# Rebuilding the last stage of a backward kernel: where dh1 is summed, when dQ and dVK are reloaded, who computes the LayerNorm backward, and when the dmod part runs

## The chip, the cores and the metric

The kernel runs on one core of one Trainium2 chip. The metric is the time of one execution on the device, in microseconds (us). A time is the median of a number of executions, which is given with it ("median of 3 runs"). The engines are PE (matmul), DVE (vector), ACT (scalar), POOL (GpSimd) and SP (which here only issues transfers). In this program PE writes its sums to tiles in PSUM; the other tiles on the chip lie in SBUF. A profile is one execution seen by the hardware profiler; its span is up to 12 us away from the median of the timed runs, so times are compared between timed runs, and stages between profiles. The kernel before took 3349.34 us (median of 3 runs, 3345.37 to 3352.89) before the change was tried.

## The reference

The program computes a transformer block with adaptive LayerNorm (attention with 32 heads of width 16, then an MLP with squared ReLU) on 2048 tokens of width 512, and then all its gradients. Cut to what the change touches:

```python
mod = (_silu(c) @ w_mod).reshape(c.shape[0], 6, 1, -1)       # sa, ca, ga, sb, cb, gb
h = _layernorm(x, axis=-1) * (1 + ca) + sa
x = x + ga * _A_ref(h, A_wqkv, A_wo)                          # attention: qkv = h @ wqkv, ...
h = _layernorm(x, axis=-1) * (1 + cb) + sb
x = x + gb * _B_ref(h, B_w1, B_b1, B_w2, B_b2)
...
_out, _vjp = jax.vjp(_f, A_x, A_wqkv, A_wo, B_w1, B_b1, B_w2, B_b2, c, w_mod)
```

The last stage of the backward pass has dQ, dK and dV of all heads and must still make five things: dh1 = dQKV · wqkvᵀ (2048 x 512), the LayerNorm backward of dh1 (which gives dx, an output, and two row sums for the gradients of sa and ca), dWqkv = h1ᵀ · dQKV, dW_mod (an outer product, 512 x 3072) and dc (which needs w_mod transposed).

## The kernel before

The attention backward walks over 8 head groups of 4 heads. It leaves dQ of a head group as a tile of 128 x 2048 (channels on the partitions, padded) in DRAM, and dV and dK together as another. The stage after that loop, which I call the tail, read them back one head group at a time:

```python
stgJ = ph.enter_context(tc.tile_pool(name="phJs", bufs=1))
...
for hg in range(HG):                                # 8 head groups
    xs = []
    for t3 in range(2):                             # dQ, dVK
        xt = stgJ.tile([P, n], BF, name=f"xst{t3}", tag=f"xst{t3}")
        SP.dma_start(out=xt[:], in_=srcs[t3][hg])
        xs.append(xt)
    for qt in range(TT):                            # 16 token tiles
        pt = pst.tile([P, 2, P], BF, name="ptq", tag="ptq")
        for t3 in range(2):
            PE.transpose(pt[:, t3, :], xs[t3][:, qt * P:(qt + 1) * P], identb[:])
        for t3 in range(3):                         # token-major dQ, dK, dV
            ...                                     # ACT copies dQ, DVE copies dK and dV
        pd = psd.tile([P, D], F32, name="pdh1", tag="pdh1")
        for t3 in range(2):
            PE.matmul(pd[:], xs[t3][:, qt * P:(qt + 1) * P], wT_pad[:, t3 * 8 + hg, :],
                      start=(t3 == 0), stop=(t3 == 1))
        if hg == 0:
            ACT.activation(dh1acc[:, qt, :], pd[:], AF.Identity)
        else:
            DVE.tensor_tensor(dh1acc[:, qt, :], dh1acc[:, qt, :], pd[:], ALU.add)
for t in range(TT):                                 # LayerNorm backward, all of it on DVE
    ...
    DVE.tensor_tensor_reduce(out=dxn1[:], in0=dh1acc[:, t, :], in1=ca1_bc, ...)
    DVE.tensor_tensor_reduce(out=prod1[:], in0=dxn1[:], in1=xn1[:], ...)
    PE.matmul(prow_sa[0:1, :], ones_bf[:, 0:1], dxn1[:], start=(t == 0), stop=(t == TT - 1))
    PE.matmul(prow_ca[0:1, :], ones_bf[:, 0:1], prod1[:], start=(t == 0), stop=(t == TT - 1))
    ...                                             # six more DVE operations, store of dx
...
SP.dma_start(out=h1J[:], in_=h1_st[:])              # then dWqkv: 192 matmuls
...                                                 # then the dmod part:
SP.dma_start(out=out_9.rearrange("(ic p) j -> p ic j", p=P), in_=dwmod_sb[:])   # 3 MB
for jc in range(24):
    SP.dma_start(out=wmodT[:, jc, :], in_=w_mod[:, jc * P:(jc + 1) * P], transpose=True)
```

Of the kernel before, what the change touches and what calls it, by code (L numbers as in the profile page):

```python
# [15 lines left out]
ALU = mybir.AluOpType  # L16
# [6 lines left out]
DC = 4  # L23
# [11 lines left out]
def kernel(  # L35
# [653 lines left out]

    with ExitStack() as ph:  # L690
        strm = ph.enter_context(tc.tile_pool(name="phIs", bufs=2))
        ework = ph.enter_context(tc.tile_pool(name="phIe", bufs=4))
        tpool = ph.enter_context(tc.tile_pool(name="phIt", bufs=2))
        stg = ph.enter_context(tc.tile_pool(name="phIg", bufs=2))
# [66 lines left out]
        def v_quad(u):  # L761
            hg, kc, qc, qi = units[u]
            qt = qc * 4 + qi
            E_u, dS_u = bst.pop(u)
            acc = cur["vk"]
            for hq in range(4):
                PE.matmul(acc[32 * hq:32 * hq + DH, :], dOs_tok[:, qt, (hg * 4 + hq) * DH:(hg * 4 + hq + 1) * DH], E_u[:, hq, :],  # L767
                          start=False, stop=(qt == TT - 1), tile_position=(0, 32 * hq), skip_group_check=True)
            if qt == TT - 1:
                ACT.activation(hst[hg]["vk"][:, kc * 512:(kc + 1) * 512], acc[:], AF.Identity)  # L770
                if kc == QC - 1:
                    SP.dma_start(out=dVKtP[hg], in_=hst[hg]["vk"][:])

        def dq_quad(b, kt):
# [9 lines left out]
            if kt == 3:  # L784
# [13 lines left out]
                if kc == QC - 1 and qc == QC - 1:  # L798
                    SP.dma_start(out=dQtP[hg], in_=st["dq"][:])
# [4 lines left out]
        with tc.manual_schedule(engines={PE.engine, ACT.engine, DVE.engine}):  # L804
            for j in range(2 * NU + 10):
                u, pair, sub = j // 2, j % 2, j % 8
                if j < 2 * NU:
                    if pair == 0 and units[u][1:] == (0, 2, 0) and units[u][0] + 1 < HG:
                        load_head(units[u][0] + 1)
                    for hi in range(2):  # L810
# [14 lines left out]
    with ExitStack() as phq:  # L825
        bigJ = phq.enter_context(tc.tile_pool(name="phJbig", bufs=1))
        dqkv_tok = bigJ.tile([P, TT, 3 * D], BF, name="dqkv_tok")
        ph = ExitStack().__enter__()
        bigJ2 = ph.enter_context(tc.tile_pool(name="phJbig2", bufs=1))
        stgJ = ph.enter_context(tc.tile_pool(name="phJs", bufs=1))  # L830
        wk = ph.enter_context(tc.tile_pool(name="phJw", bufs=2))
        dh1acc = bigJ2.tile([P, TT, D], F32, name="dh1acc")
        x0_tok = bigJ2.tile([P, TT, D], BF, name="x0_tokJ")
        SP.dma_start(out=x0_tok[:], in_=x_dram)
        dx1_tok = bigJ2.tile([P, TT, D], BF, name="dx1_tokJ")
        SP.dma_start(out=dx1_tok[:], in_=dx1_st[:])
        with ExitStack() as ph2:
            pst = ph2.enter_context(tc.tile_pool(name="psJt", bufs=2, space=bass.MemoryType.PSUM))
            psd = ph2.enter_context(tc.tile_pool(name="psJd", bufs=2, space=bass.MemoryType.PSUM))
            srcs = (dQtP, dVKtP)  # L840
            for hg in range(HG):
                xs = []
                for t3 in range(2):
                    xt = stgJ.tile([P, n], BF, name=f"xst{t3}", tag=f"xst{t3}")
                    SP.dma_start(out=xt[:], in_=srcs[t3][hg])
                    xs.append(xt)
                for qt in range(TT):
                    pt = pst.tile([P, 2, P], BF, name="ptq", tag="ptq")
                    for t3 in range(2):
                        PE.transpose(pt[:, t3, :], xs[t3][:, qt * P:(qt + 1) * P], identb[:])  # L850
                    for t3 in range(3):
                        dst = dqkv_tok[:, qt, t3 * D + hg * 64:t3 * D + (hg + 1) * 64].rearrange("q (h d) -> q h d", h=4)
                        srcv = pt[:, 0 if t3 == 0 else 1, :].rearrange("q (h c) -> q h c", h=4)
                        srcv = srcv[:, :, DH:2 * DH] if t3 == 1 else srcv[:, :, 0:DH]
                        if t3 == 0:
                            ACT.activation(dst, srcv, AF.Identity)
                        else:
                            DVE.tensor_copy(dst, srcv)
                    pd = psd.tile([P, D], F32, name="pdh1", tag="pdh1")
                    for t3 in range(2):  # L860
                        PE.matmul(pd[:], xs[t3][:, qt * P:(qt + 1) * P], wT_pad[:, t3 * 8 + hg, :],
                                  start=(t3 == 0), stop=(t3 == 1))
                    if hg == 0:
                        ACT.activation(dh1acc[:, qt, :], pd[:], AF.Identity)
                    else:
                        DVE.tensor_tensor(dh1acc[:, qt, :], dh1acc[:, qt, :], pd[:], ALU.add)
        with tc.tile_pool(name="psJr", bufs=1, space=bass.MemoryType.PSUM) as psr:
            prow_sa = psr.tile([P, D], F32, name="prow_sa")
            prow_ca = psr.tile([P, D], F32, name="prow_ca")
            for t in range(TT):  # L870
                xn1 = wk.tile([P, D], BF, name="xn1b", tag="xn1b")
                DVE.tensor_scalar(xn1[:], x0_tok[:, t, :], mean1[:, t:t + 1], rstd1[:, t:t + 1], ALU.subtract, ALU.mult)
                dxn1 = wk.tile([P, D], BF, name="dxn1", tag="dxn1")
                s1 = wk.tile([P, 1], F32, name="s1a", tag="s1a")
                DVE.tensor_tensor_reduce(out=dxn1[:], in0=dh1acc[:, t, :], in1=ca1_bc, scale=1.0, scalar=0.0,
                                         op0=ALU.mult, op1=ALU.add, accum_out=s1[:])
                prod1 = wk.tile([P, D], BF, name="prod1", tag="prod1")
                s2 = wk.tile([P, 1], F32, name="s2a", tag="s2a")
                DVE.tensor_tensor_reduce(out=prod1[:], in0=dxn1[:], in1=xn1[:], scale=1.0, scalar=0.0,
                                         op0=ALU.mult, op1=ALU.add, accum_out=s2[:])  # L880
                PE.matmul(prow_sa[0:1, :], ones_bf[:, 0:1], dxn1[:], start=(t == 0), stop=(t == TT - 1))
                PE.matmul(prow_ca[0:1, :], ones_bf[:, 0:1], prod1[:], start=(t == 0), stop=(t == TT - 1))
                c1 = wk.tile([P, 1], F32, name="c1a", tag="c1a")
                DVE.tensor_scalar(c1[:], s1[:], 1.0 / D, None, ALU.mult)
                c2 = wk.tile([P, 1], F32, name="c2a", tag="c2a")
                DVE.tensor_scalar(c2[:], s2[:], 1.0 / D, None, ALU.mult)
                tq = wk.tile([P, D], BF, name="tqa", tag="tqa")
                DVE.tensor_scalar(tq[:], xn1[:], c2[:, 0:1], None, ALU.mult)
                uq = wk.tile([P, D], BF, name="uqa", tag="uqa")
                DVE.tensor_tensor(uq[:], dxn1[:], tq[:], ALU.subtract)  # L890
                vq = wk.tile([P, D], BF, name="vqa", tag="vqa")
                DVE.tensor_scalar(vq[:], uq[:], c1[:, 0:1], rstd1[:, t:t + 1], ALU.subtract, ALU.mult)
                dx0t = wk.tile([P, D], BF, name="dx0t", tag="dx0t")
                DVE.tensor_tensor(dx0t[:], dx1_tok[:, t, :], vq[:], ALU.add)
                SP.dma_start(out=out1_v[:, t, :], in_=dx0t[:])
            rowt2 = wk.tile([1, 2, D], F32, name="rowt_saca", bufs=1)
            DVE.tensor_copy(rowt2[:, 0, :], prow_sa[0:1, :])
            DVE.tensor_copy(rowt2[:, 1, :], prow_ca[0:1, :])
            SP.dma_start(out=rows_st[0:2, :].unsqueeze(0), in_=rowt2[0:1, :, :])
        ph.__exit__(None, None, None)  # L900
        bigJ3 = phq.enter_context(tc.tile_pool(name="phJbig3", bufs=1))
        wk = phq.enter_context(tc.tile_pool(name="phJw2", bufs=2))
        h1J = bigJ3.tile([P, TT, D], BF, name="h1J")
        SP.dma_start(out=h1J[:], in_=h1_st[:])
        with tc.tile_pool(name="psJw", bufs=1, space=bass.MemoryType.PSUM) as psw:
            for t3 in range(3):
                accs = [psw.tile([P, D], F32, name=f"awq_{ic}", tag=f"awq_{ic}") for ic in range(DC)]
                for t in range(TT):
                    for ic in range(DC):
                        PE.matmul(accs[ic][:], h1J[:, t, ic * P:(ic + 1) * P], dqkv_tok[:, t, t3 * D:(t3 + 1) * D],  # L910
                                  start=(t == 0), stop=(t == TT - 1))
                for ic in range(DC):
                    wblk = wk.tile([P, D], BF, name="wqblk", tag="wqblk")
                    ACT.activation(wblk[:], accs[ic][:], AF.Identity)
# [114 lines left out]
```

## Time and profile before

| stage, kernel before | us | length | what holds it |
|---|---|---|---|
| attention backward loop, end | 3047.4 | | last dQ sum on POOL |
| wait for the first reload | 3047 to 3062 | 14.5 | the last dQ goes out and comes back |
| transposes and dh1, 128 steps | 3062 to 3197 | 135 | see below |
| LayerNorm backward | 3197 to 3244 | 47 | DVE |
| wait for h1 | 3244 to 3254 | 10 | DMA |
| dWqkv | 3254 to 3300 | 46 | PE |
| dmod part | 3300 to 3345 | 45 | transfers, DVE, PE in turn |

The tail is 298 us. The page's first part (busy time and share of the span of each engine) doesn't show it, since the tail is 9% of the span:

```profile
PE 2615.0 (78%) x17549; PEld 775.1 (23%) x17549; DVE 2004.4 (60%) x2889; ACT 2151.9 (64%) x3457; POOL 442.9 (13%) x458
```

So the tail has to be read by stretches. Each row of the next view is one stretch of time: its length, then the busy time of each engine (and the count of its instructions), the granted PE clock (1.00 is full speed), the share of the DMA engines and the rate. It is the view by windows of the kernel before.

```profile
core 0: us, PE busy (x) PEld busy (x) DVE busy (x) ACT busy (x) POOL busy (x), PEclk, DMA share, GB/s
3062.00:3197.00 135.00, 101.16 (x512) 46.10 (x510) 94.44 (x367) 35.56 (x144) 0.00 (x0) 0.87 0.16 55
3197.00:3244.00 47.00, 18.10 (x32) 2.52 (x32) 47.00 (x177) 0.00 (x0) 0.00 (x0) 0.54 0.12 39
3244.00:3254.00 10.00, 0.30 (x1) 0.14 (x2) 8.30 (x7) 0.00 (x0) 0.00 (x0) 0.50 0.63 236
3254.00:3300.00 46.00, 43.90 (x192) 19.15 (x190) 0.00 (x0) 5.48 (x11) 0.00 (x0) 0.95 0.09 29
3300.00:3345.00 45.00, 20.63 (x72) 6.39 (x72) 10.50 (x37) 14.06 (x26) 0.00 (x0) 0.61 0.51 147
```

In no row but the LayerNorm backward (DVE 47.00 of 47 us) and dWqkv (PE 43.90 of 46) is an engine busy all or nearly all the time. In the first row PE is busy for 101 us of 135 and DVE for 94. The waits of PE in that stretch (total us, times, longest):

```profile
PE ptq L850 <- DMA xst_31730<-dQtP: 16.6, 1, 16.6
PE ptq L850 <- DMA xst_31894<-dQtP: 3.7, 1, 3.7
PE ptq L850 <- DMA xst_32222<-dQtP: 3.5, 1, 3.5
...
PE ptq L850 <- DMA xst_32550<-dQtP: 3.3, 1, 3.3
...
```

There is one stop at the start of each head group, because each of the two tiles has one buffer, which is refilled only when the last step of the group before has read it. Between the stops, the timeline of DVE shows a step (start, duration, instruction):

```profile
3102.36 0.28 DVE L858 COPY dqkv_tok<-ptq 128x64 bf16<-128x64 bf16 x2
3102.56 0.68 DVE L866 TENSOR_TENSOR dh1acc<-dh1acc,pdh_32118 128x512 f32<-128x512 f32 x1
3103.16 0.28 DVE L858 COPY dqkv_tok<-ptq 128x64 bf16<-128x64 bf16 x2
3103.36 0.67 DVE L866 TENSOR_TENSOR dh1acc<-dh1acc,pdh_32128 128x512 f32<-128x512 f32 x1
```

While a sum on POOL runs, an addition of the same shape on DVE takes 0.95 us, and 0.41 us when none runs (minimum, median, maximum in ns):

```profile
L510 DVE TENSOR_TENSOR x_c<-ftmp,x_c x16: 413/948/953, 703.9 to 1560.9; 128x512 bf16<-128x512 bf16 x16
```

### The profile page before, as it was taken

The numbers are of one execution on the slowest core, as the hardware profiler recorded it, in microseconds if no ns is written. First come the engines' busy times: TensorE is split into PE (matmuls) and PEld (weight loads), VectorE is DVE, ScalarE is ACT, GpSimd is POOL, SyncE is SP. The second block draws the span as 40 slices with busy tenths as digits, with TensorE's granted clock in tenths as the row PEclk, the third lists the DMA queues.
The fourth block names the chain that finished last, engine by engine and source line by source line (L and its number), as shares of the span: only waits on it lengthen the run. The fifth ranks groups of instructions, "written<-read, shape, count | busy, mean of one in ns | idle before, by whom it ended". The sixth has DMA issues, their size and how long they took to land.

```text
span 3345.0 us, 47765 instructions
## 1 busy us (share of the span) xinstructions
PE 2615.0 (78%) x17549; PEld 775.1 (23%) x17549; DVE 2004.4 (60%) x2889; ACT 2151.9 (64%) x3457; POOL 442.9 (13%) x458
## 2 busy tenths in 40 slices
PE   2778998887787887474798878888888988896746
PEld 1222111222222222131122222222222222222312
DVE  8952002343443443345687878788887878884781
ACT  0005999897896988300686878777777878884202
POOL 3000001022133122313010110101010101010000
PEclk7976555897798799686787889888887888887867
DMA  4125001446439347886999999999999999996113
GB/s 153 57 96 158 29 28 40 100 117 172 77 85 183 81 94 147 125 161 207 192 199 214 198 211 198 213 201 208 204 197 209 199 215 198 202 199 166 62 63 95
DMA packets 1399560, 497.70 MB, mean 149 GB/s; under 512 B 1324051, under 2 KB 1363735, under 8 KB 1398813
## 3 DMA queue, kind: packets, MB, share of 16 engines
q1 hardware_dynamic: 1370430, 467.38, 69.8%
q0 software_dynamic: 12384, 25.17, 4.2%
q10 hardware_dynamic: 16512, 2.10, 0.5%
q8 instruction: 138, 2.26, 0.3%
q14 instruction: 96, 0.79, 0.1%
HBM read 95.51 MB, written 78.27 MB: 52 GB/s over the span
## 4 chain that ended last, share of the span: by engine, by line
PE 34%; DMA 24%; ACT 16%; DVE 12%; issue 8%; SPq 4%; POOL 1%; DVEq 0%; POOLq 0%; ACTq 0%
DMA dsT<-dS_u 16%; ACT ET L580 11%; PE psS_u L730 6%; ACT E_u L732 5%; PE dqacc L782 5%; PE accVK L767 3%; PE ppad L270 3%; PE accVK L758 2%; PE psST L578 2%; DVE dS_u L744 2%; DMA dw_st<-dwp 2%; PE psS_x L730 2%; PE pm L417 2%; PE pm L437 1%; PE pm L499 1%
## 5 line engine op out<-in xcount | busy, mean ns | idle before, releaser
L744 DVE TENSOR_TENSOR dS_u<-psD_u,E_u 128x1024 bf16<-128x1024 f32 x1024 | 1188.8, 1216 | 262.0 <-PE psD_u L742 167.1
L732 ACT ACTIVATE E_u<-psS_u 128x512 bf16<-128x512 f32 x1536 | 868.2, 635 | 303.7 <-PE psD_u L742 277.0
L580 ACT ACTIVATE ET<-psST 128x1024 bf16<-128x1024 f32 x1024 | 948.9, 1260 | 133.6 <-PE psST L578 133.1
L730 PE MATMUL psS_u<-ik,iq 32*128 32x512 bf16 x1536 | 518.2, 434 | 17.2 <-DMA ik<-KtP 7.4
L742 PE MATMUL psD_u<-iv,ido 32*128 32x512 bf16 x2048 | 447.9, 432 | 38.2 <-DVE dS_u L744 22.5
L578 PE MATMUL psST<-qt_sb,kt_sb 32*128 32x512 bf16 x2048 | 399.4, 477 | 65.8 <-ACT ET L580 30.6
L782 PE MATMUL dqacc<-dsT,KS_tok 128*32 128x512 bf16 x2048 | 214.8, 507 | 164.0 <-DMA dsT<-dS_u 139.4
L732 ACT ACTIVATE E_u<-psS_x 128x512 bf16<-128x512 f32 x512 | 334.4, 653 | 12.5 <-PE psD_u L742 10.2
L594 PE MATMUL oacc<-ET,vaug 128*32 128x512 bf16 x2048 | 253.2, 485 | 1.3 <-DVE ostage L598 1.3
L767 PE MATMUL accVK<-E_u,dOs_tok 128*16 128x512 bf16 x2048 | 226.6, 432 | 0.0
L730 PE MATMUL psS_x<-ik,iq 32*128 32x512 bf16 x512 | 210.2, 411 | 0.3
L797 POOL TENSOR_TENSOR dQacc<-dQacc,dqtmp 128x512 f32<-128x512 f32 x64 | 81.0, 1266 | 848.4 <-ACT dqtmp L792 848.4
L730 PEld LDWEIGHTS <-iq 32*128 32x128 bf16 x2048 | 98.8, 93 | 368.6 <-issue 368.4
L742 PEld LDWEIGHTS <-ido 32*128 32x128 bf16 x2048 | 124.4, 93 | 248.8 <-issue 215.0
L598 DVE COPY ostage<-oacc 128x512 f32<-128x512 f32 x32 | 21.9, 686 | 261.3 <-PE oacc L594 261.3
L578 PEld LDWEIGHTS <-kt_sb 32*128 32x128 bf16 x2048 | 83.3, 94 | 403.5 <-issue 392.7
L347 DVE COPY dwp<-pm 128x512 f32<-128x512 f32 (+1 forms) x102 | 67.2, 659 | 176.8 <-PE pm L340 98.2
L340 PE MATMUL pm<-tk,h_c 128*128 128x512 bf16 (+1 forms) x256 | 71.4, 409 | 63.7 <-DVE dwp L347 52.7
L758 PE MATMUL accVK<-dS_u,qz_12963 128*32 128x512 bf16 x1024 | 113.3, 431 | 7.8 <-ACT vkb L770 7.1
L758 PE MATMUL accVK<-dS_u,qz_12962 128*32 128x512 bf16 x1024 | 111.9, 427 | 7.2 <-ACT vkb L770 7.2
L270 PE MATMUL ppad<-xn1T,wpadT 128*128 128x512 bf16 x384 | 100.2, 411 | 20.9 <-DVE stagep L273 16.2
L782 PEld LDWEIGHTS <-KS_tok 128*32 128x32 bf16 x2048 | 52.2, 106 | 225.3 <-issue 179.3
(1022 smaller groups left out, 2563.9 us busy)
## 6 DMA issues: line engine op xcount, KB each, us to landing
dw_st<-dwp POOLq DMA_DIRECT2D x90, 256.0 KB, 4.8
kt_sb<-KtP SPq DMA_DIRECT2D x32, 512.0 KB, 3.6
dsT<-dS_u SPq DMA_TRANSPOSE x512, 4.9
dwp<-dw_st SPq DMA_DIRECT2D x30, 256.0 KB, 3.0
wA<-in_B_w_dram SPq DMA_DIRECT2D x4, 1792.0 KB
wB<-in_B_w_dram SPq DMA_DIRECT2D x4, 1792.0 KB
QtP<-stagep SPq DMA_DIRECT2D x8, 512.0 KB, 2.8
KtP<-stagep SPq DMA_DIRECT2D x8, 512.0 KB, 2.6
```

Source lines behind the costliest of these rows:

```text
L270: PE.matmul(pp[:], wpadT[:, ic, which, hg, :], h1T[:, ic, qc * 512:(qc + 1) * 512], start=(ic == 0), stop=(ic == DC - 1))
L578: PE.matmul(ps[:, hi, :], kt_sb[r:r + 32, kt * P:(kt + 1) * P], qt_sb[r:r + 32, :], start=True, stop=True, tile_position=(r, 0))
L580: ACT.activation(ET[:, 2 * pair:2 * pair + 2, :], ps[:], AF.Exp, scale=SCALE)
L594: PE.matmul(oacc[32 * hq:32 * hq + 32, :], lhsT, ET[:, hq, :], start=(kt == 0), stop=(kt == TT - 1), tile_position=(0, 32 * hq), skip_grou ...
L730: PE.matmul(psS[:], st["q"][r:r + 32, qt * P:(qt + 1) * P], st["k"][r:r + 32, kc * 512:kc * 512 + 512], start=True, stop=True, tile_positi ...
L732: ACT.activation(bst[u][0][:, hq, :], psS[:], AF.Exp, scale=SCALE)
L742: PE.matmul(psD[:, hi, :], st["do"][r:r + 32, qt * P:(qt + 1) * P], st["v"][r:r + 32, kc * 512:kc * 512 + 512], start=True, stop=True, til ...
L744: DVE.tensor_tensor(dS_u[:, 2 * pair:2 * pair + 2, :], psD[:], E_u[:, 2 * pair:2 * pair + 2, :], ALU.mult)
L758: PE.matmul(cur["vk"][32 * hq:32 * hq + 32, :], hst[hg]["qz"][:, qt, hq, :], bst[u][1][:, hq, :], start=(qt == 0), stop=False, tile_positi ...
L767: PE.matmul(acc[32 * hq:32 * hq + DH, :], dOs_tok[:, qt, (hg * 4 + hq) * DH:(hg * 4 + hq + 1) * DH], E_u[:, hq, :], start=False, stop=(qt ...
L782: PE.matmul(acc[32 * hq:32 * hq + 32, :], KS_tok[:, kc * 4 + kt, h * DH:h * DH + 32], tT[:, :, hq * 4 + kt, :], start=(kt == 0), stop=(kt ...
L797: POOL.tensor_tensor(dst2, dst, tmp[:], ALU.add)
```

## The change

Its intent is to keep PE fed through the whole tail. dh1 of a token tile is now summed over all head groups by 16 matmuls into one PSUM bank, so DVE adds nothing. For that, all 16 tiles of dQ and dVK must be on chip at once: those of the last head groups stay there (dVK of two groups and dQ of one, which are no longer stored), four (head groups 0 and 1) are reloaded during the last head group of the loop, and the rest right after it. The LayerNorm backward of tile t runs under the dh1 matmuls of later tiles: ACT makes the normalised x, DVE the rest, POOL keeps the running sums for the two rows. The dmod part is cut in two, columns 2 to 5 in the middle of the LayerNorm stage, columns 0 and 1 (which need the row sums) between two groups of dWqkv matmuls. The diff, cut to its core:

```diff
+    def load_grads(hg, pool, tags):
+        for key, dsrc, tag in (("dq", dQtP, tags[0]), ("vk", dVKtP, tags[1])):
+            if (hg, key) not in xs:
+                xs[hg, key] = pool.tile([P, n], BF, name=f"x{key}", tag=tag)
+                SP.dma_start(out=xs[hg, key][:], in_=dsrc[hg])
...                                                  # in the loop, in the last head group:
+                    if pair == 0 and units[u] == (HG - 1, 2, 0, 0):
+                        load_grads(0, strm, ("iq", "ik"))
+                        load_grads(1, strm, ("iv", "ido"))
...                                                  # the tail
-            for hg in range(HG):                    # all of the 128 steps shown above
...
+        for k, hg in enumerate(order):              # transposes, four token tiles at a time
+            for g in range(TT // 4):
+                pt = pst.tile([P, 2, 4, P], BF, name="ptq", tag="ptq")
...
+        for t in range(TT):
+            if t == 2:
+                load_wmodT(2)
+                load_wmodT(3)
+            if t == 8:
+                dmod_part((2, 3, 4, 5), True, False)
...
+            pd = psd.tile([P, D], F32, name="pdh1", tag="pdh1")
+            for k, hg in enumerate(order):
+                for i, key in enumerate(("dq", "vk")):
+                    PE.matmul(pd[:], xs[hg, key][:, t * P:(t + 1) * P], wT_pad[:, i * 8 + hg, :],
+                              start=(k == 0 and i == 0), stop=(k == HG - 1 and i == 1))
+            ACT.activation(xn1[:], x0s[t // 2][:, t % 2, :], AF.Identity, bias=nb1[:, t:t + 1], scale=rstd1[:, t:t + 1])
...
+            for j, rsrc in ((0, dxn1), (1, prod1)):
+                if t == 0:
+                    POOL.tensor_copy(rsum[:, j, :], rsrc[:])
+                else:
+                    POOL.tensor_tensor(rsum[:, j, :], rsum[:, j, :], rsrc[:], ALU.add)
...
+        for b in range(3):
+            for ic in range(DC):
+                dwqkv(b, ic)                        # 16 matmuls
+                if (b, ic) == (1, 0):
+                    rowsa = {}
+                    for j in range(2):
+                        pr = psd.tile([P, D], F32, name="prs", tag="pdh1")
+                        PE.matmul(pr[0:1, :], onesf[:, 0:1], rsum[:, j, :], start=True, stop=True)
+                        rowsa[j] = pr
+                    dmod_part((0, 1), False, True)
```

## The prediction

> **What bounds the kernel now.** The timeline shows the attention-backward loop ending at 3047.4 us (last dQ sum on POOL). The tail after it ends at 3345.0: 298 us, a row of stages with one limit each:
>
> - 3047–3062: PE idle; the last dQ goes out and returns behind 4 MB of x and dx1 (chain of waits: DMA xst<-dQtP, 13.5 us).
> - 3062–3197: 128 steps (8 head groups x 16 token tiles). Busy time by windows: DVE 15.6 of 20 us, PE 14.8. Each step puts two 64-column copies (0.18 us) and the f32 dh1 addition (0.67 us) on DVE; PE also waits 3.5 to 5 us for xst at each head group.
> - 3197–3244: LN backward, DVE 20.0 of 20 us, granted clock 0.50.
> - 3244–3254: PE waits for h1J.
> - 3254–3300: dWqkv, clock 1.00, 192 matmuls.
> - 3300–3345: dmod part; 24 weight transposes on the SP queue, 1.26 us each, then a 3 MB store.
>
> **What the change does.** It removes 112 DVE additions (75 us busy), three full stops of PE and the serial dmod part. Kept on PE: 256 transposes (0.11 us with weight load), 256 dh1 and 192 dWqkv matmuls at 0.215 us (warm spacing in the trace), dmod matmuls: 28+55+41+13, about 137 us warm. The scheduler interleaves transposes and dh1 matmuls and puts 16 transposes before the last dqacc.
>
> **What is given back (estimates).**
>
> 1. Four 512 KB reloads move into the last head group. A group with loads took 178.6 us between dVK stores, the last, without, 170.4: I expect +6 us in the loop, whose pace the transposes in the SP queue set.
> 2. LN: DVE 2.3 us per tile is below PE's 16 x 0.215 = 3.45. But POOL now adds two 128x512 f32 sums per tile (1.15 to 1.26 us each in the trace). The Trainium skill, "SBUF — State Buffer", in its list of engine ports, says that DVE instructions with two SBUF inputs contend with GpSimd reads and that one then fully blocks. The trace agrees: an L510 addition took 0.88 instead of 0.41 us while a POOL sum ran. So 4.2 to 4.6 us per tile where it isn't hidden: +10 us.
> 3. dmod: four reciprocals of 3.3 us. The second part (columns 0, 1) sits in the PE order between dWqkv groups and waits for DVE, then for single-buffered stores: 15 us.
> 4. Cold clock and loads of groups 2 to 6: 5 us.
>
> Tail from 3047: 26 (remaining transposes) + 52 (dh1) + 10 + 8 (first dmod part) + 5 + 41 + 15 + 5 (cold clock, last eviction and store) = 162; loop +6. Span about 3215, time about 3219 us (run times lie 2 to 4 us above the span). All of it is on the critical path: nothing else runs in the tail.
>
> **Prediction: 3219 us, range 3195 to 3250; 0.97 faster by over 2%, 0.025 within 2%, 0.005 slower.**
>
> **What would show it.** Busy time by windows: PE over 16 of 20 us and clock near 0.9 from about 3055 on, with one hole in dWqkv. DVE lines: no dh1 additions; prod, subtract and final LN instructions longer than 0.68/0.42/0.68 us where POOL runs. dVK stores: last head group about 176 us. Waits: PE on dxn (PSUM buffer) in the LN stage; PE idle 10 to 15 us at the two row sums.
>
> **What would make it wrong.** POOL and DVE not blocking each other (10 us less); SP, in order, stuck on a load that waits for a buffer, starving DVE of dx1 and so PE (10 to 30 us more); the loop losing more than 6 us through loads queued before the last transposes; the start of the loop moving, since the first head group's loads are reordered (I expect none: it waits for the wT_pad transposes anyway).

## More of the kernel before

A step lasts 0.80 us and DVE fills it without a gap: inside a head group DVE sets the pace.

## The result, and the profile after

The changed kernel took 3230.26 us (median of 4 runs, 3227.02 to 3232.93), the kernel before 3351.11 us (4 runs, 3345.37 to 3354.6; the three quoted at the start are among them). The ratio is 0.964, with a 95% interval of 0.962 to 0.966. Ratios here are the mean time of one kernel's runs over that of the other's of the same rounds, so they are not quite the ratio of the medians that I quote. The gain is 121 us. The result passed the comparison with the reference, which is a loose one (see e2 and b2).

The loop, measured from the store of dVK of head group 5 to the end of the last dQ sum, became longer: 362.9 us against 355.1. The tail, from there to the end, became 168.1 us against 297.7. So 130 us were won in the tail and 8 given back in the loop. The windows of the changed kernel, with the columns as before:

```profile
3058.00:3080.00 22.00, 20.08 (x231) 14.52 (x232) 17.04 (x43) 11.76 (x29) 4.07 (x4) 0.99 1.04 318
3080.00:3100.00 20.00, 16.49 (x106) 8.46 (x104) 17.40 (x37) 3.77 (x10) 8.84 (x6) 1.00 0.38 100
3100.00:3120.00 20.00, 17.25 (x74) 5.54 (x72) 20.00 (x31) 7.24 (x12) 12.92 (x9) 0.83 0.27 85
3120.00:3140.00 20.00, 15.00 (x46) 4.05 (x45) 10.53 (x19) 4.05 (x7) 4.99 (x5) 0.84 0.67 139
3140.00:3160.00 20.00, 19.10 (x79) 8.02 (x78) 16.70 (x27) 5.50 (x8) 7.89 (x7) 0.90 0.36 118
3160.00:3178.00 18.00, 18.00 (x83) 7.82 (x82) 9.99 (x17) 2.76 (x6) 4.61 (x4) 1.00 0.17 59
3178.00:3196.00 18.00, 9.31 (x30) 2.25 (x28) 5.54 (x5) 4.74 (x10) 0.00 (x0) 0.69 0.14 52
3196.00:3225.00 29.00, 25.29 (x111) 11.00 (x109) 0.00 (x0) 4.61 (x14) 0.00 (x0) 0.96 0.13 41
```

The same line of the page shows almost none of it: PE's share rose from 78 to 80% because the span fell, and its busy time fell by only 33 us.

```profile
PE 2582.1 (80%) x17521; PEld 767.2 (24%) x17521; DVE 1944.8 (60%) x2480; ACT 2141.8 (66%) x3369; POOL 486.2 (15%) x490
```

In the windows, PE works from the first microseconds of the tail at full clock, and the stages no longer follow each other: the LayerNorm backward lies under the dh1 matmuls. Two weak places remain, around 3100 to 3140 and from 3178 to 3196. The second is the hole in dWqkv that I had expected at the row sums. Its timeline on DVE, and what PE then waits for:

```profile
3178.53 0.68 DVE L894 TENSOR_TENSOR dmodbf<-prs,inv 1x512 bf16<-1x512 f32 x1 [7.92 <-PE prs L1009]
3179.24 3.34 DVE L893 RECIPROCAL inv<-modbc 1x512 f32<-1x512 bf16 x1
3182.69 0.68 DVE L894 TENSOR_TENSOR dmodbf<-prs,inv 1x512 bf16<-1x512 f32 x1
...
```

```profile
3183.43 0.26 PE L898 MATMUL pcolK<-ones_bf,dmodbf 1*128 1x1 bf16 x4 [3.66 <-DVE dmodbf L894]
3192.13 1.06 PE L911 MATMUL pwm<-dmodbf,siluc_rowbfK 1*128 1x512 bf16 x2 [2.36 <-ACT dwm L912]
3195.38 1.01 PE L989 MATMUL pwq<-dvk_tok,h1J 128*128 128x512 bf16 x2 [2.18 <-ACT dwm L912]
```

In the waits of PE over the whole tail, the 16.6 us and the stops at each head group are gone. The largest entries belong to the dmod part, and DVE in the LayerNorm stage (s12a) is a small one:

```profile
PE pwm L911 <- ACT dwm L912: 6.0, 4, 2.4
PE pcolK L898 <- DVE dmodbf L894: 3.7, 1, 3.7
...
PE pdh_32356 L957 <- DVE s12a L963: 2.4, 1, 2.4
...
```

The last dWqkv matmul before the hole ends about 3177.5, and the next starts at 3195.4: 17.9 us. A reciprocal of 512 numbers on one partition takes 3.34 us and PE waits for it; later ACT may not write the next dW_mod tile until the single buffer's store has landed (ACT waits 4.3 us in two stops for out_dram<-dwm), and PE waits for ACT. PE does not stand still for all of the 17.9 us: it is busy for 9.2 of them with the dmod part's own matmuls, at a granted clock of 0.71, and its waits for DVE (3.7) and ACT (4.9) sum to 8.6.

The blocking of DVE by POOL, expected in the prediction, is plain in the timeline of the steady part (DVE first, then POOL):

```profile
3160.22 0.68 DVE L963 CUSTOM_DVE_ANT_0 dxn_32777<-pdh_32758,modbc 128x512 bf16<-128x512 f32 x1
3161.09 1.67 DVE L966 CUSTOM_DVE_ANT_0 prod_32780<-dxn_32777,xn1b 128x512 bf16<-128x512 bf16 x1 [0.17 <-DVE s12a L963]
3163.01 1.21 DVE L976 TENSOR_SCALAR tqa<-xn1b,c12a 128x512 bf16<-128x512 bf16 x1
3164.25 0.42 DVE L978 TENSOR_TENSOR uqa<-dxn_32777,tqa 128x512 bf16<-128x512 bf16 x1
```

```profile
3161.06 1.15 POOL L972 TENSOR_TENSOR rsum<-rsum,dxn_32777 128x512 f32<-128x512 f32 x1 [2.15 <-DVE s12a L963]
3162.91 1.15 POOL L972 TENSOR_TENSOR rsum<-rsum,prod_32780 128x512 f32<-128x512 f32 x1 [0.70 <-DVE s12a L966]
```

The product (two inputs in SBUF) starts 0.03 us after POOL's sum and takes 1.67 instead of 0.68 us; the scalar operation starts 0.10 us after the second sum and takes 1.21 instead of 0.40 us. Both end 0.2 to 0.6 us after POOL does. The first DVE instruction, whose first input lies in PSUM, took 0.67 to 0.69 us in all 16 tiles, also at 3097.85 us, where it ran wholly inside a POOL sum. This agrees with the Trainium skill, "SBUF — State Buffer", section "Who interferes with whom": a DVE instruction with two SBUF inputs contends with a GpSimd instruction that reads SBUF, one in a mode that uses both port pairs contends too (scalar operations can enter such a mode), and the later one waits for the whole instruction of the other; a DVE instruction with at most one SBUF input, outside these modes, does not contend. That the scalar operation here ran in such a mode is inferred from its wait.

### The profile page after: what moved, and what is told of

It reads as the page before. It is cut to its first block, busy times and chain, and to the rows that moved or that the text cites. A ratio compares the mean times of both kernels' runs of the same rounds, so it can differ in the third digit from the quotient of the medians.

```text
span 3225.2 us, 47200 instructions
## 1 busy us (share of the span) xinstructions
PE 2582.1 (80%) x17521; PEld 767.2 (24%) x17521; DVE 1944.8 (60%) x2480; ACT 2141.8 (66%) x3369; POOL 486.2 (15%) x490
## 4 chain that ended last, share of the span: by engine, by line
PE 36%; DMA 24%; ACT 17%; DVE 11%; issue 7%; SPq 4%; POOL 1%; DVEq 0%; ACTq 0%; POOLq 0%
DMA dsT<-dS_u 16%; ACT ET L580 11%; PE psS_u L739 7%; PE dqacc L794 5%; ACT E_u L741 5%; PE accVK L776 3%; PE ppad L270 3%; PE accVK L767 2%; PE psST L578 2%; PE psS_x L739 2%; DVE dS_u L753 2%; PE pm L417 2%; PE pm L499 1%; PE pm L437 1%; PE pwq L989 1%
```

## The experiments

I had eleven runs in three groups (a0, e1, e2 and e3; e6, b1, best1 and best2; b2, b3 and best3), each group on one chip with its own runs of the kernel before (medians 3350.85, 3349.08 and 3348.64 us). The last two groups were on the same chip, the first on another. "Tail" and "loop" are the two lengths defined above, read from each run's profile.

| run | median us | ratio to before, 95% interval | loop us | tail us |
|---|---|---|---|---|
| kernel before (first profile) | 3351.11 | 1 | 355.1 | 297.7 |
| changed kernel (first profile) | 3230.26 | 0.964 [0.962, 0.966] | 362.9 | 168.1 |
| a0, changed kernel again | 3227.72 | 0.964 [0.961, 0.966] | 363.6 | 170.6 |
| e1, reloads after the loop | 3227.45 | 0.964 [0.961, 0.967] | 352.7 | 180.5 |
| e2, without POOL sums | 3222.91 | 0.963 [0.960, 0.965] | 361.9 | 167.2 |
| e3, dmod at the end | 3241.08 | 0.968 [0.966, 0.970] | 363.0 | 184.6 |
| e6, reloads issued from ACT | 3231.95 | 0.966 [0.964, 0.967] | 360.8 | 170.8 |
| b1, before with two buffers | 3322.45 | 0.992 [0.990, 0.993] | 355.8 | 264.2 |
| b2, before without additions | 3330.03 | 0.995 [0.992, 0.997] | 354.7 | 272.7 |
| b3, b1 and b2 together | 3284.32 | 0.981 [0.978, 0.983] | 355.6 | 232.7 |
| best1 | 3210.10 | 0.959 [0.956, 0.961] | 363.1 | 151.5 |
| best2 | 3209.19 | 0.958 [0.955, 0.960] | 364.1 | 146.4 |
| best3 | 3210.81 | 0.959 [0.956, 0.962] | 360.6 | 146.5 |

My theory was the sum in the prediction: the tail follows PE's work, with four costs on top (reloads in the loop, DVE blocked by POOL, the hole in dWqkv, the first dmod part). The rivals were that one of these costs is not real, and that the sum in PSUM, the change's first item, is not what wins.

### a0: the changed kernel again

No edit. It fixes the scatter between profiles of one kernel: 2.5 us in the tail, 0.7 us in the loop, 2.5 us in the median.

> The changed kernel unchanged, as the base for the other runs on this chip: ratio to the kernel before 0.962 to 0.966; in its profile the tail from the last dQ sum on POOL to the end takes 168 us plus or minus 3.

Measured: 3227.72 us (3221.64 to 3231.59), tail 170.6, loop 363.6. Differences of less than about 3 us in a stage say nothing from one profile.

### e1: the four reloads after the loop

```diff
-                    if pair == 0 and units[u] == (HG - 1, 2, 0, 0):
-                        load_grads(0, strm, ("iq", "ik"))
-                        load_grads(1, strm, ("iv", "ido"))
...
+        load_grads(0, strm, ("iq", "ik"))
+        load_grads(1, strm, ("iv", "ido"))
         load_grads(2, strm, ("iq", "ik"))
...                                          # and, in load_grads, before the transfer:
+                if hg < 2:
+                    POOL.tensor_copy(xs[hg, key][:, 0:1], xs[HG - 1, "vk"][:, n - 1:n])
```

A one-column copy from the last result of the loop into each tile makes the load wait (POOL has nothing else to do there), and the transfer overwrites the column.

> The four 512 KB reloads of head groups 0 and 1 wait for the end of the loop instead of running inside the last head group. My theory (the reloads slow the loop, whose pace the transposes in the SP queue set): from the fifth-but-last dVK store (group 5) to the last dQ sum the loop takes 354 to 357 us, as in the kernel before (355), instead of 363 in the changed kernel; in return PE waits in the tail for 2 MB more, 7 us at 300 GB/s, so the whole time stays within 3 us of the changed kernel. Rival (the reloads cost the loop nothing and the 8 us come from the order of the last two transposes behind another load, or from chance): the loop stays at 363 and the time rises by 7 us or more.

Measured: the loop became 10.9 us shorter than in a0 (352.7 against 363.6) and the tail 9.9 us longer (180.5 against 170.6). The time is the same, 3227.45 against 3227.72 us. The early reload costs in the loop what it saves in the tail. So the loss in the loop is real and caused by these loads, and this part of the change is worth nothing that shows.

### e6: the same reloads from another queue

```diff
-                        load_grads(0, strm, ("iq", "ik"))
-                        load_grads(1, strm, ("iv", "ido"))
+                        load_grads(0, strm, ("iq", "ik"), ACT)
+                        load_grads(1, strm, ("iv", "ido"), ACT)
```

It tells apart why the loop loses: slots in SP's queue, where every load stands between transposes (which, by my prediction, set the pace), or the bytes.

> The changed kernel with the four reloads inside the last head group issued by the ACT queue instead of the SP queue. From the dVK store of group 5 to the last dQ sum the changed kernel takes 363 us, the one with late reloads 353, the kernel before 355. Theory SP slots (my prediction: the transposes in the SP queue set the pace, and each load takes 0.6 to 1.3 us of that queue): 359 us or less. Rival, bandwidth (the 16 DMA engines are busy all the time in the loop, 2 MB at about 200 GB/s cost 10 us whoever issues them): 362 to 364 us. Whole time: within 4 us of the changed kernel either way.

Measured: loop 360.8 us, 2.8 us less than in a0 and still 5 to 8 us more than in the kernels without the reload (352.7 to 355.8). That lies between the two expectations (359 or less, 362 to 364), so neither was met. The size of the effect holds: the six profiles with the reload on SP's queue have 361.9 to 364.1 us, the two with it on ACT's (e6 and best3) 360.8 and 360.6. The time did not move (3231.95, interval of the ratio 0.964 to 0.967). So about a third of the loss, at most, is the queue. The rest goes with the loads whichever queue issues them; that it is their 2 MB on a path that the loop's transposes already fill is likely (the windows of the kernel before give the loop 201 to 206 GB/s, at which 2 MB take about 10 us, an estimate, and a DMA share above 1), but no run tests the bytes alone. One of these windows:

```profile
2680.00:2860.00 180.00, 152.65 (x1268) 42.49 (x1264) 147.72 (x128) 139.57 (x276) 17.96 (x13) 0.88 1.14 205
```

### e2: without the sums on POOL

```diff
             for j, rsrc in ((0, dxn1), (1, prod1)):
                 if t == 0:
                     POOL.tensor_copy(rsum[:, j, :], rsrc[:])
-                else:
-                    POOL.tensor_tensor(rsum[:, j, :], rsum[:, j, :], rsrc[:], ALU.add)
```

The row sums are wrong (columns 0 and 1 of dmod; the comparison still passed, so it does not guard these values closely).

> POOL sums only the first token tile (dmod rows 0 and 1 are wrong on purpose). Both theories expect the LN instructions of DVE at 0.68 (prod), 0.40 (scale), 0.42 (subtract) and 0.75 us (final) instead of 1.67, 1.20, up to 1.36 and up to 1.63, and about 3 us per tile instead of 5.15. Theory of the prediction: blocking is on the critical path, so 10 us are saved. Rival, from the trace of the changed kernel (PE waited for DVE in the LN stage only 5 us in all, and the lag at the end hides behind the first dWqkv blocks): 2 to 5 us are saved.

The groups of DVE instructions in the tail, first of the changed kernel, then of this run (count, then busy us and mean ns):

```profile
L976 DVE TENSOR_SCALAR tqa<-xn1b,c12a 128x512 bf16<-128x512 bf16 x16 | 14.4, 899 | 0.3
L980 DVE SCALAR_TENSOR_TENSOR dx1J<-uqa,rstd_83,dx1J 128x512 bf16<-128x512 bf16 x16 | 14.2, 889 | 0.3
L974 DVE TENSOR_SCALAR c12a<-s12a 128x2 f32<-128x2 f32 x16 | 7.1, 443 | 0.2
```

```profile
L974 DVE TENSOR_SCALAR tqa<-xn1b,c12a 128x512 bf16<-128x512 bf16 x16 | 6.4, 401 | 0.3
L978 DVE SCALAR_TENSOR_TENSOR dx1J<-uqa,rstd,dx1J 128x512 bf16<-128x512 bf16 x16 | 11.9, 746 | 0.3
L972 DVE TENSOR_SCALAR c12a<-s12a 128x2 f32<-128x2 f32 x16 | 2.6, 165 | 0.2
```

Every blocked instruction came back to its own length, so the blocking is shown. Yet the time fell only from 3227.72 to 3222.91 us, 4.8 us, and the intervals of the two ratios overlap: the gain is not clear of noise. It fits the rival (2 to 5 us) and not my theory (10). The stage from the end of the loop to the first dWqkv matmul stayed at 102.3 us, against 102.9 and 106.0 for the changed kernel. DVE lost its extra work, but other waits had the same length: the timeline of e2 still shows DVE idle for 7.23 us before one of its tiles, waiting for PE. The cost is real on the engine and, as far as the time shows, mostly not on the critical path.

### e3: the dmod part at the end

```diff
-            if t == 8:
-                dmod_part((2, 3, 4, 5), True, False)
-                load_wmodT(0)
-                load_wmodT(1)
...
-                    dmod_part((0, 1), False, True)
+        dmod_part((2, 3, 4, 5), True, False)
+        dmod_part((0, 1), False, True)
```

> Both dmod parts are moved behind the last dWqkv block, nothing else. Theory A (the early place hides the dmod work): the time rises by 25 us or more, since the stage took 45 us at the end of the kernel before. Theory B (in PE's fixed order the early place only moves the wait: 18 us hole at the second part, some 20 us of waits and slow clock around the first): the LN stage is 15 to 20 us shorter, the hole goes, the end is 30 to 38 us longer, and the time changes by less than 6 us.

Measured: 3241.08 us, 13.4 us more than a0. That is between the two theories (25 or more, less than 6): both missed. The dWqkv matmuls, but for four that the scheduler placed earlier, started 89.3 us after the end of the loop (102.9 and 106.0 in the two profiles of the changed kernel) and had no hole of more than 2.1 us, but behind the last of them came 51 us of dmod, where the changed kernel has 4; theory B had expected 30 to 38 more. The edit did not move all of it: the trace of e3 still has two reciprocals on DVE (at 3089.78 and 3106.37 us) and the loads of their rows in the LayerNorm stage. With PE's part gone from there, PE's waits for DVE (s12a) grew to 15.7 us in 9 stops, from 3.3 and 5.6 in the two profiles of the changed kernel. The windows of this last stretch:

```profile
3196.00:3216.00 20.00, 9.97 (x19) 1.56 (x18) 0.68 (x1) 3.27 (x6) 0.00 (x0) 0.50 0.51 132
3216.00:3239.00 23.00, 7.14 (x14) 1.19 (x12) 0.00 (x0) 7.69 (x15) 0.00 (x0) 0.50 0.23 91
```

No engine is busy for half of the time. The early place hides only 13 us of a part that takes about 50 alone: most of it is paid again as the hole of 17.9 us and as 14 to 17 us in the LayerNorm stage. Is that the work, or its order? This led to best1.

### b1: two buffers in the kernel before

```diff
-        stgJ = ph.enter_context(tc.tile_pool(name="phJs", bufs=1))
+        stgJ = ph.enter_context(tc.tile_pool(name="phJs", bufs=2))
```

> The kernel before with two buffers for each of the two reloaded gradient tiles, so that the next head group's load runs under the present group's work; nothing else changed. If the waits at the seven later head groups are PE's own loss, 7 x 3.5 us = 24 us are saved, ratio to the kernel before 0.992 to 0.994, and the stage of 136 us takes about 111. Rival (the stage is bound by DVE, so that PE's waits are filled by what DVE has still to do): less than 8 us saved.

Measured: 3322.45 us, a ratio of 0.992, or 28 us less. The stops between head groups are gone; the only wait for xst left is the first, 16.5 us. One number of one line was worth 28 us, where the whole change is worth 121. It is also more than the 24 us that I had expected: the stage fell from 134.9 to 101.7 us, not to 111. A stop costs more than its wait. In the last head group of the kernel before, the first three steps after the stop are 1.24, 1.44 and 1.01 us apart and the later ones 0.79 or 0.80 (starts of the dh1 matmuls in the trace); the granted clock of the stage is 0.87, against 1.00 in the steady windows of b1. The Trainium skill, "Perfetto Trace Analysis", section "Optimization Strategy", says that the same gap repeating on the engine that should be saturated can mean that there is no room for the next tile; the seven stops of 3.3 to 3.7 us agree.

### b2 and b3: what the sum in PSUM is worth

The additions on DVE are taken away and nothing put in their place, so dx is wrong (only the first head group reaches dh1acc; the comparison passed here too). In b3 the stops for the buffers are gone as well.

```diff
                     if hg == 0:
                         ACT.activation(dh1acc[:, qt, :], pd[:], AF.Identity)
-                    else:
-                        DVE.tensor_tensor(dh1acc[:, qt, :], dh1acc[:, qt, :], pd[:], ALU.add)
```

> The kernel before, with the 112 DVE additions of dh1 taken away and nothing else (dx is wrong on purpose: only head group 0 reaches dh1acc). It measures what the DVE half of the dh1 sum is worth alone. Theory (the adds were hidden behind PE and behind the stops for xst): in 3062 to 3197 PE was busy 101 us of 135 and waited 24 us for xst at seven group starts, so there is little to win while these stops stay: the stage falls from 135 to 123 to 130 us, the time to 3337 to 3345. The stops for xst stay at 3 to 4 us each. Rival (the adds set the pace, as their 75 us of busy time suggest): the time falls by 40 us or more, to about 3300.

> The kernel before with two xst buffers (as b1, which gained 28 us) and without the 112 additions (wrong on purpose). In b1's steady stage DVE was busy 20.0 of 20 us and PE 17.7 at clock 1.00, 26 steps in 20 us (0.78 us a step). Theory: without additions PE sets the pace at about 0.69 us a step, so 128 steps lose 10 to 14 us against b1: time 3308 to 3314. Rival (additions and stops hide each other, so that both together are worth much more than the sum): 3295 or less.

Measured: b2 took 3330.03 us (ratio 0.9945, 18 us less), b3 3284.32 us (0.9805, 65 us less). For b2 both expectations missed: it won more than my theory allowed (3337 to 3345) and far less than the rival's 40 us. For b3 my theory was wrong (3308 to 3314) and the rival's bound was met (3295 or less). The length of the stage of 128 steps, from the first transpose to the end of the last dh1 matmul, shows how: 134.9 us before, 101.7 in b1, 113.7 in b2, 74.3 in b3. The stops are worth 33 us with the additions in place and the additions 21 with the stops in place; the sum is 54, both together are 61. So the two costs nearly add up, with 6 us more for both. The 6 us are in the stops, which cost 39 us without the additions (113.7 to 74.3): the steps after a stop of b2 are 0.96 to 1.3 us apart too, and what they lose is larger against a steady step of 0.54 than against one of 0.79. The timed differences (28, 18 and 65 us) are coarser: the point from which the loop is measured lay between 2692.2 and 2702.9 us in these four profiles, before any of the edits. Where my estimate went wrong is in these windows, b1 first, then b3:

```profile
3100.00:3120.00 20.00, 17.64 (x102) 8.61 (x101) 20.00 (x78) 5.69 (x26) 0.00 (x0) 1.00 0.17 54
```

```profile
3100.00:3120.00 20.00, 20.00 (x149) 11.25 (x148) 10.66 (x74) 8.19 (x37) 0.00 (x0) 1.00 0.31 107
```

In b1, PE was busy 17.64 of 20 us with 102 matmuls, and I concluded that it could do hardly more: 0.69 us a step. Freed of DVE it did 149 matmuls in the same 20 us, 0.54 us a step. The busy time of pipelined matmuls is not the time that they need. The Trainium skill, "Perfetto Trace Analysis", section "Identifying the Most-Contended Engine", warns of it (the matmul busy share is not a good measure of how close PE is to its limit; it names the share of the weight loads, beside the work done, to be used instead). The trace agrees: the weight loads went from 8.61 to 11.25 us, up by 31%, while the matmuls rose by 46% in number and by 13% in busy time. The count of matmuls in a window is the measure that told the truth.

### best1: the dmod part in another order

```diff
-        for b in range(3):
-            for ic in range(DC):
-                dwqkv(b, ic)
-                if (b, ic) == (1, 0):
...
-                    dmod_part((0, 1), False, True)
+        inv_cb = wk.tile([1, D], F32, name="inv", tag="inv", bufs=2)     # two reciprocals instead of four, written
+        DVE.reciprocal(inv_cb[:], modbc[0:1, 4, :])                      # behind the LayerNorm loop
...
+        jobs = [(10, job_pcol, ((2, 3, 4, 5),))]       # the dmod part in pieces of one to eight matmuls
...
+                if t % 4 == 3:                         # in dwqkv: after every fourth matmul
+                    slot[0] += 1
+                    if jobs and jobs[0][0] <= slot[0]:
+                        _, f, args = jobs.pop(0)
+                        f(*args)
...
+        with tc.manual_schedule(engines={PE.engine, ACT.engine}):        # keep this order on PE and ACT
+            for b in range(3):
+                for ic in range(DC):
+                    dwqkv(b, ic)
```

Also, dW_mod is stored from ACT's queue, from three buffers that the LayerNorm stage no longer needs.

> The changed kernel with the whole dmod part taken out of the LN stage and spread in small pieces between groups of four dWqkv matmuls (fixed PE and ACT order), two reciprocals instead of four, dmod-weight stores issued by ACT. My theory (the two dmod parts cost 30 us of waits because PE, SP and DVE work in order, and not because of their work): LN stage from the last dQ sum to the first dWqkv matmul 87 to 93 us instead of 103 to 106, dWqkv stage with all pieces 53 to 58 us instead of 59 to 60, no hole above 3 us, tail 146 to 155 us instead of 168 to 171, ratio to the kernel before 0.956 to 0.960. Rival (the waits come back: pieces wait for DVE, which lags behind in the LN stage because POOL blocks it): tail 160 us or more, ratio 0.961 or more.

Measured: 3210.10 us, 17.6 us less than a0 (on another chip) and 21.9 less than e6, which ran beside it; the intervals of best1 and e6 do not meet (0.956 to 0.961, 0.964 to 0.967). The first dWqkv matmul starts 86.9 us after the loop (102.9 and 106.0 in the changed kernel), and PE has no hole from there to the end:

```profile
3133.00:3153.00 20.00, 20.00 (x101) 7.71 (x100) 11.51 (x20) 6.14 (x11) 5.03 (x5) 1.00 0.24 81
3153.00:3173.00 20.00, 20.00 (x80) 5.95 (x78) 0.00 (x0) 8.16 (x17) 0.00 (x0) 1.00 0.67 180
```

The stage of dWqkv took 61.0 us, as in the changed kernel (61.3 and 60.7) and not the 53 to 58 expected; but it now holds all of PE's dmod work, where the changed kernel has a third of it (24 of 72 matmuls) and the hole. So most of what e3 showed as paid again was not PE's work but its place and its waits. It is not quite the same work, though: the trace has both reciprocals at 1560.0 and 1564.4 us, long before the tail, where the changed kernel has three in the tail (10 us of DVE). No run tells apart the order, the reciprocals, the extra buffers and the other queue. best2, below, has both reciprocals in the tail again (at 3059 and 3063 us) and is no slower. In the waits of PE in this tail one large entry is left, and it is DVE in the LayerNorm stage, which POOL slows down (e3 had the same wait, 15.7 us):

```profile
PE pdh L920 <- DVE s12a L926: 13.7, 9, 1.6
```

### best2 and best3

best2 takes the sums from POOL: PE adds them up in PSUM with two matmuls against a column of ones per token tile, as the kernel before did.

```diff
-                if t == 0:
-                    POOL.tensor_copy(rsum[:, j, :], rsrc[:])
-                else:
-                    POOL.tensor_tensor(rsum[:, j, :], rsum[:, j, :], rsrc[:], ALU.add)
+                PE.matmul(prow[j][0:1, :], ones_bf[:, 0:1], rsrc[:], start=(t == 0), stop=(t == TT - 1))
```

> As the spread-dmod kernel, and the two row sums are made by PE in PSUM (32 more matmuls, 6.9 us) instead of by POOL, so that nothing blocks DVE in the LN stage. If POOL's blocking is hidden there (PE needs 78 us for the LN stage, DVE at 5.15 us per tile 82), this gives nothing: LN stage 86 to 92 us, ratio within 0.0015 of the spread-dmod kernel. If the blocking is what binds the LN stage once dmod is gone, the LN stage falls below 86 us and the time by 4 us or more.

Measured: 3209.19 us, a ratio of 0.9575 [0.955, 0.960]. The wait of 13.7 us is gone: the waits of PE in the tail now sum to 2.8 us. But 32 matmuls were added, and the tail is 146.4 against 151.5 us. Both expectations are half met: the first dWqkv matmul comes 82.8 us after the loop (86.9 in best1), as if the blocking had bound that stage, but the time is the same within the scatter of either (3196 to 3214, and 3200 to 3220 us). In timed runs best1 and best2 can't be told apart. The windows show what limits the tail now (two of them):

```profile
3100.00:3120.00 20.00, 20.00 (x87) 7.52 (x86) 14.51 (x36) 4.06 (x5) 0.00 (x0) 1.00 0.28 85
3120.00:3140.00 20.00, 20.00 (x85) 7.21 (x84) 15.23 (x40) 3.25 (x4) 0.00 (x0) 1.00 0.14 47
```

best3 is best2 with the edit of e6.

> best2 (209 us class: 3209.2) with the four reloads in the loop issued from the ACT queue, as in e6, where the loop lost 2 to 3 us less but the time did not move (3232 against 3228). Theory: within the scatter, 3205 to 3212. Rival (SP queue slots matter once the tail is short): 3203 or less.

Measured: 3210.81 us, the same. All three beat both kernels: about 140 us under the kernel before, 17 to 21 under the change.

## Why the prediction was right

It predicted 3219 us with a range of 3195 to 3250 and came out at 3230. The direction and the size were right, and the sum was 11 us short. Point by point:

**The tail as a chain of stages with one limit each: right.** All the gain appeared where it was expected, 130 us in the tail.

**The sum of the tail, 162 us: 6 to 9 us short.** Measured were 168.1 and 170.6. That it came so close is in part luck: the term for the first dmod part was about 7 us too small and the term for the LayerNorm stage some 5 us too large. The terms, where the runs measured them:

- *"dmod ... The second part ... waits for DVE, then for single-buffered stores: 15 us."* The mechanism was right in both halves; the hole was 17.9 us, 8.6 of them waits and 9.2 PE's own work.
- *"8 (first dmod part)."* Too small. Without either part before it, dWqkv started 14 to 17 us sooner (e3), and with the part spread 16 to 19 us sooner (best1, 86.9 against 102.9 and 106.0). So about 15 us, not 8. It is the part on PE and ACT, with its waits, that costs this: the two reciprocals of 3.3 us on DVE, and in SP's queue the loads of single rows that stand behind eight weight transposes, were in the LayerNorm stage of e3 as well.
- *"LN: ... 4.2 to 4.6 us per tile where it isn't hidden: +10 us."* The blocking was there, and larger than I said (two tiles in a row were 5.16 us apart on DVE), but its cost was about 5 us at most (e2: 4.8, not clear of noise). Its place in the sum was wrong: in this kernel other waits covered most of it. When PE's dmod work left the stage, PE's waits for DVE there rose to 15.7 us (e3) and 13.7 us (best1).

**"+6 us in the loop, whose pace the transposes in the SP queue set": size about right, cause mostly wrong.** The loop grew by 8 us. e1 shows that the reloads cause it, and e6 and best3 that only about 3 us of it come from the queue that they were issued on.

**"All of it is on the critical path: nothing else runs in the tail": right for the total, but it says nothing of what each part was worth.** From the experiments, the 130 us of the tail divide like this. About 33 us are the stops for single buffers (b1: 297.7 to 264.2). About 32 more are the additions on DVE (b3: to 232.7), 27 of them in the stage of 128 steps. About 13 us, perhaps, are the early dmod part (e3, measured the other way round: 13.4 us in time, 14 in the tail). About 25 us are the two waits for transfers that PE no longer has (14.5 before the first transpose and 10 for h1, read from the trace and tested by no run); the reloads that do away with the first one, though, cost the loop 8. That is 103 of 130; the remaining 27 us are probably the LayerNorm backward, which now lies under the dh1 matmuls; that is a subtraction, and no run tests it alone.

**The item the change is named for was not the largest single one in reach.** The prediction listed "112 DVE additions (75 us busy)" as removed. What they cost was 21 to 27 us of stage (b2 alone, b3 against b1), because the work PE had to do anyway ran beside them. Busy time removed is not time won: here it was about three times the gain in the stage. In the timed runs the gain was 18 and 37 us, which the scatter leaves uncertain by about 10.

**The signs named beforehand.** PE over 16 of 20 us and a clock near 0.9: right in most windows, not in 3120 to 3140 (15.0) and in the hole. No dh1 additions, and longer DVE instructions where POOL runs: right. PE waiting on DVE in the LayerNorm stage: hardly (2.4 us the longest), which fits e2. PE idle 10 to 15 us at the row sums: the hole was longer, 17.9 us, but the idle time in it shorter, 8.6 us.

**Run noise.** In the first profile of the changed kernel, a point before anything had changed (the last operation of the MLP's backward, start 1560.88 us before) lay 4.6 us later, at 1565.51. At the store from which the loop is measured, 2.0 us of this were left (2694.2 against 2692.2). So of the 10 us by which that profile's span of 3225 missed the 3215 I had written, 2 were there before the loop's last two groups, 2 are the loop's growth over the expected 6, and 6 the tail.

What stays open: whether the loop's loss is bandwidth alone, and how the last 27 us of the tail divide.

## What to carry to other kernels

Ask of each engine's busy time what it would be without the others: a count of instructions per window, compared with the best window of the same work, shows a waiting engine that its busy share hides. Moving work under another stage pays only in the order in which the engines meet it: here the dmod part cost about 18 us more until it was cut into small pieces, with its inputs ready before PE reaches them, two reciprocals fewer and more buffers for its stores. And look for repeating stops on a single buffer before rebuilding a stage; that one-line change alone was worth 28 us, where the whole rebuild is worth 121.

## What the Trainium skill lacked or had wrong

- "SBUF — State Buffer", "Who interferes with whom": the rule agreed with the cases looked at here. What it lacks is a duration for small compute instructions, which pay as much as large ones: a scalar operation on 128 x 2 numbers, 0.15 to 0.17 us alone, took 1.11 us in four of 16 tiles beside POOL's sums, and its mean fell from 443 to 165 ns when they were taken away. POOL loses too: its sums of 1.15 us took up to 2.59 us. The longest, from 3098.89 us, lasts across three DVE instructions in a row (from 3098.87, 3099.47 and 3099.79) that kept their own length, though two of them start after it (spans on POOL are rough in this profile).
- "VectorE: DVE Perf Modes", "First, the fixed hardware budget": it says that a reciprocal is an iterative divide with a repeat count of 8, but gives no duration. Here 512 numbers on one partition took 3.34 us, against 0.68 us for a two-input operation of the same shape, and PE waited 3.66 us for one.
- "Perfetto Trace Analysis", "Identifying the Most-Contended Engine": right that the busy share of matmuls misleads, and the runs agree with its reason, that pipelined instructions look smaller (0.134 us of busy time per matmul in b3, 0.173 in b1, where DVE holds PE up). What it lacks is a size, and the consequence for an engine that is held up: b1's PE read as 88% busy while it did 102 of the 149 matmuls that b3 did in 20 us.
- No page that I read says what a load costs a loop whose windows already show a DMA share above 1 (1.14 to 1.16): four loads of 512 KB made it 8 to 11 us longer, and the queue that issued them changed that by about 3 us.
